# Five buffers for the last batch's layer norm, and `moe2_w_k` rebuilt by column halves

## The chip, the cores and the metric

The kernel runs on one core of a Trainium2 chip. Its engines are TensorE (PE in the profile, its weight loads PEld), VectorE (DVE), ScalarE (ACT), GpSimd (POOL) and SyncE (SP), whose queue issues nearly all DMAs. Each engine works through its own list of instructions in order; they meet only through semaphores. The metric is the time of one execution in microseconds (us) on the device; the median of several runs counts, lower is better.

## The reference, cut to what matters

Batch 4, 8 heads, 576 positions, head size 64, so the model width is 512. An attention with a decay is followed by two blocks of matrix products:

```python
x = attention(q, k, v, f)                      # (4, 576, 512) after joining the heads
h = relu(x @ w_in)                             # 512 -> 1024
u, v = h[..., :512], h[..., 512:]
v_n = (v - mean(v)) / sqrt(var(v) + 1e-6)      # layer norm over the 512 columns
v_s = einsum('ts,bsd->btd', w_spatial, v_n) + b_spatial[None, :, None]
x = (u * v_s) @ w_out                          # 512 -> 512
x_prev = x shifted by one position, zero at the start of each batch
xk = mu_k * x + (1 - mu_k) * x_prev
xr = mu_r * x + (1 - mu_r) * x_prev
k = relu(xk @ w_k)                             # 512 -> 1024
out = sigmoid(xr @ w_r) * ((k * k) @ w_v)      # 1024 -> 512
```

The inputs of the second block are `moe2_mu_k`, `moe2_mu_r`, `moe2_w_k`, `moe2_w_v` and `moe2_w_r`, those of the first `moe_w_in`, `moe_w_spatial`, `moe_b_spatial` and `moe_w_out`. The profile leaves the 2 of moe2 out: `moe_w_k` in a row is `moe2_w_k`. Matrices come in 64-bit floats, read as pairs of 32-bit integers.

## The kernel before, in words

**Order of the work.** The program gives each piece of work a due time and sorts by it (`add`, `run`, lines 612 to 619). That fixes the program order; from it a scheduler of the language, with a timeline of its own, makes each engine's fixed list, so that an instruction whose inputs and buffers come late can be placed behind later ones. An instruction given to `pin` (line 59) is never placed ahead of the one traced before it on its engine.

**First block, batch by batch.** `plan_mlp` (lines 592 to 608) plans three groups of products for a batch: `m1v` (line 499), the `v` half of x @ w_in, in five blocks of rows (four of 128, the last of 64); `m1u` (line 559), the `u` half, in 8 tiles of 128x288; `m2` (line 572), the product with `w_spatial`, also 8 tiles, each the sum of 14 matmuls (line 585): 12 on the four full row blocks `vn`, 2 on `v0`, which holds the fifth. For batch 3, the last, the 42 halves are spread over 4.0 units of time instead of 7.0, since no attention work is left.

Each row block has a layer norm in four steps. `ln1` (line 518) takes a buffer `vt` of 128x512 and a small one, `mv`, from the pool `acts`, and ScalarE reads the product out of PSUM into `vt` with a relu (line 522). `ln2` (line 525): VectorE's statistics (lines 529, 530), ScalarE's logarithm and exponential of the variance (533, 534), five small GpSimd operations that refine the result (535 to 539). `ln3` (line 541): VectorE scales `vt` in place (544), ScalarE copies it to float16 (549; 546 and 547 for the fifth block). `ln4` (line 551): VectorE takes the rest that the float16 copy leaves (557; 555 for the fifth block). `vt` comes free when `ln4` has read it. With `bufs=2` in

```python
        v = w.tile([128, 512], F32, tag="vt", bufs=2, name="vt")
        mv = w.tile([128, 4], F32, tag="mv", bufs=3, name="mv")
```

there are two `vt` and three `mv`. In the last batch the products of `m1v` lie in PSUM banks that the attention used (lines 502 to 505), two and two. The end of `m2` is line 588 on VectorE, which multiplies by `u` out of PSUM; line 590 stores the result to HBM (`gd`).

**Second weights.** `weights2` (line 665) is a generator. Each step fetches the block after next to come (512 KB, SP queue, line 93, two buffers `wst`) and rebuilds the present one: `raw_convert` (line 96) makes 32-bit floats on ScalarE (100) and VectorE (103, 107, 108), with 100 and 103 pinned; `split` (line 63) makes a high part on ScalarE (64) and the rest on VectorE (65). A fetch buffer comes free after line 108. The list of blocks is made at line 677: a block is 128 rows (`kc`) by 512 columns, so `moe_w_out` has 4, `moe2_w_k` 8, `moe2_w_r` 4 and, in a second generator, `moe2_w_v` 8 (one for each row block `fc`). For `moe2_w_k` the rows are the outer loop, the two column halves the inner one.

**The end of the batches** is in `body`. At line 819 everything up to the last batch's products is traced; `attn`, the big pool on the right, is released, the pools of the second weights are opened there, and the loop of lines 829 to 832 puts one weight block behind each 0.22 units of the last batch's steps. Then the PSUM pools and the left pools are released (line 833), and the third stage starts.

**Third stage.** 2304 tokens in five chunks of 512 (the last 256). For each chunk `m3` (line 704) multiplies the stored `gd` by `moe_w_out`, four tiles of 12 matmuls; `mix` (728) makes `xk` and `xr`, split in two; `chunk` (748) has eight products `m4(fc)` with `moe2_w_k`, each over its four row blocks and the 128 columns of `fc` (line 758), eight `m5(fc)` with `moe2_w_v` (fc is its row block) and the gate with `moe2_w_r`. The next chunk's `m3` and `mix` are interleaved as `side`. All these matmuls are recorded under line 726.

Of the kernel before, what the change touches and what calls it, by code (L numbers as in the profile page):

```python
# [7 lines left out]
F32 = mybir.dt.float32  # L8
# [13 lines left out]
KB = [(128 * c, 128) for c in range(4)] + [(512, 64)]  # L22
# [20 lines left out]
class K:  # L43
# [472 lines left out]
            self.vp[j] = self.m1p  # L516

    def ln1(self, b, j):
        w, tn = self.acts, KB[j][1]
        v = w.tile([128, 512], F32, tag="vt", bufs=2, name="vt")  # L520
        mv = w.tile([128, 4], F32, tag="mv", bufs=3, name="mv")
        self.nc.scalar.activation(v[:tn], self.vp.pop(j)[:tn], AF.Relu, scale=self.ds[:tn, 1:2])
        self.vv[j] = (v, mv)

# [87 lines left out]
    def add(self, t, prio, fn, *args):  # L612
        self.steps.append((t, prio, len(self.steps), fn, args))
# [51 lines left out]
    def weights2(self, p, names, stage, pin=False):  # L665
        nc, a = self.nc, self.a
        if not hasattr(self, "mu"):
            self.w2 = {}
            mu = self.mu = p.tile([128, 2, 2, 4], F32, name="mu")
            for i, nm in enumerate(("moe2_mu_k", "moe2_mu_r")):  # L670
                nc.sync.dma_start(mu[:, i, 0], a[nm])
                nc.vector.tensor_scalar(mu[:, i, 1], mu[:, i, 0], -1.0, 1.0, op0=ALU.mult, op1=ALU.add)
        blocks = []
        for nm in names:
            rows, cn = a[nm].shape
            self.w2[nm] = p.tile([128, 2, rows // 128, cn], F32R, name=nm)
            blocks += [(nm, kc, slice(c0, c0 + 512)) for kc in range(rows // 128) for c0 in range(0, cn, 512)]

        todo = iter(blocks)
        st = {}  # L680
        def fetch():
            x = next(todo, None)
            if x:
                nm, kc, cs = x
                st[nm, kc, cs.start] = self.raw_load(stage, nm, slice(128 * kc, 128 * kc + 128), cs, nc.sync)
        fetch()
        yield
        for nm, kc, cs in blocks:
            fetch()
            e = stage.tile([128, 512], F32, tag="we", bufs=2, name="we")  # L690
            self.raw_convert(st.pop((nm, kc, cs.start)), e, pin)
            self.split(e, self.w2[nm][:, 0, kc, cs], self.w2[nm][:, 1, kc, cs])
            yield
# [99 lines left out]
def body(tc, a, out):  # L793
    k = K(tc, a, out)
    G = k.B * k.H
    k.setup()
    k.cum()
    k.plan_attention()
    for i, t in enumerate((-4.35, -2.35) + tuple(0.6 + 0.1 * x for x in range(8))):
        k.add(t, 8, k.init, i + 1)  # L800
    add = k.add
    add(0.6, 8, k.v0_init)
    for i in range(8):
        hf, kc = 1 - i // 4, i % 4
        t = (P["w1"] if hf else P["w0"]) + P["wd"] * kc
        add(t, 7, k.wconv, i)
        if i > 2:
            add(t - 1.2, 9, k.wload, i, k.nc.sync)
        add(P["s1"] + P["sd"] * kc if hf else P["s0"] + P["sd"] * kc, 7, k.wsplit, i)
    add(P["s1"] - 0.5, 7, k.wscale, 1)  # L810
    add(P["s0"] - 0.5, 7, k.wscale, 0)
    ws = k.weights_spatial()
    for i in range(9):
        add(P["wsp"] + 0.4 * i, 7, next, ws, 0)
    end = 0
    for b in range(k.B):
        end = k.plan_mlp(b, 8 * b + 8 + P["mlp"] + (0, 0, 0.8, 0)[b], P["mlplen"] if b < 3 else 4.0)
    last = G + 1.45
    k.run(last)
    k.at.release()  # L820
    wp = k.pool("weights2", side="right")
    k.p3 = k.pool("phase3", side="right")
    wst = k.pool("wstage2", side="right")
    k.chunks = [(512 * i, min(512, 2304 - 512 * i)) for i in range(5)]
    k.x2, k.xx = {}, {}
    w2 = k.weights2(wp, ("moe_w_out", "moe2_w_k", "moe2_w_r"), wst, True)
    next(w2)
    last += 1.65
    while k.steps:
        last += 0.22  # L830
        k.run(last)
        next(w2, 0)
    for p in (k.pso, k.pst, k.pss, k.psm, k.acts, k.w):
        p.release()
    k.ps3 = k.pool("ps3", space=PSUM)
    k.p2 = k.pool("phase2", side="left")
    w2b = k.weights2(k.p2, ("moe2_w_v",), wst)
    wrest = (x for w in (w2, w2b) for x in w)
    for _ in k.m3(0):
        next(w2, 0)  # L840
    for w in range(2):
        for _ in k.mix(0, w):
            next(w2, 0)
    for _ in range(4):
        next(wrest, 0)
    for i in range(5):
        side = (x for y in ((k.m3(i + 1), k.mix(i + 1, 0), k.mix(i + 1, 1)) if i < 4 else ()) for x in y)
        n = 0
        for _ in k.chunk(i):
            next(wrest, 0)  # L850
            n += 1
            if n <= 5 or n >= 9:
                next(side, 0)
            if n == 12:
                next(side, 0)
        for _ in side:
            next(wrest, 0)
    for p in (k.ps3, k.p2, wst, k.p3, wp, k.hl, k.c):
        p.release()
# [42 lines left out]
```

## Time and profile before

| | before |
|---|---|
| median of 3 runs | 744.61 us (744.12 to 744.65) |
| profiled execution: its time | 743.56 us |
| profiled execution: span from first to last instruction | 741.7 us |
| mean granted TensorE clock | 0.973 |
| TensorE busy, share of the span | 664.9 us, 90% |
| VectorE busy | 413.7 us, 56% |
| ScalarE busy | 372.1 us, 50% |
| GpSimd busy | 153.9 us, 21% |

Times in rows are us from the start of the span. "Busy" is the union of an engine's instructions; two of them can overlap a little, so a row of 0.69 us can be followed by the next 0.60 us later. The granted clock is a share of full speed: 1.00 is 2.4 GHz, 0.50 is 1.2 GHz. A wait is put down to the instruction that released it.

### The profile page before, as it was taken

What the parts mean: (1) busy time and instruction counts of PE and PEld (TensorE: products, weight loads), DVE (VectorE), ACT (ScalarE), POOL (GpSimd) and SP (SyncE); (2) the same over time, 40 slices, a digit from 0 to 9 for tenths busy, and PEclk for the clock granted to TensorE, in tenths of its full rate; (3) what the DMA queues carried; (4) which work ended last, traced back from release to release, by engine and by line L of the source; (5) the groups of instructions that cost most, each with busy time, mean ns of one, the idle gap of its engine ahead of it and who ended that gap; (6) DMA issues with size and microseconds to landing.
All of it is one profiled execution on the core that took longest, in us unless ns stands there. A gap on an engine that the chain in (4) does not pass through costs nothing.

```text
span 741.7 us, 11689 instructions
## 1 busy us (share of the span) xinstructions
PE 664.9 (90%) x4166; PEld 457.6 (62%) x4166; DVE 413.7 (56%) x1122; ACT 372.1 (50%) x762; POOL 153.9 (21%) x356
## 2 busy tenths in 40 slices
PE   1488886999989899999998489999999999999997
PEld 0234343466655565456655267788888888888896
DVE  6868776874465555553118789886226412731342
ACT  4547776595446744454317448655335322622431
POOL 8122434443335223442212000000000000000000
PEclk9999798999999999999999599999999999999999
DMA  7977566444461434400115464441000100010010
GB/s 239 256 207 184 139 119 183 150 96 104 104 167 52 115 73 107 84 18 18 50 49 196 144 198 153 142 115 47 10 29 15 57 1 15 0 57 1 0 57 30
DMA packets 73616, 70.07 MB, mean 94 GB/s; under 512 B 50883, under 2 KB 51555, under 8 KB 73558
## 3 DMA queue, kind: packets, MB, share of 16 engines
q1 hardware_dynamic: 73126, 68.14, 33.5%
q10 hardware_dynamic: 432, 1.18, 0.4%
q8 instruction: 33, 0.54, 0.3%
q14 instruction: 25, 0.20, 0.1%
HBM read 43.78 MB, written 9.79 MB: 72 GB/s over the span
## 4 chain that ended last, share of the span: by engine, by line
PE 56%; DMA 21%; DVE 8%; ACT 5%; POOL 4%; issue 3%; SPq 2%; POOLq 0%; ACTq 0%; DVEq 0%
PE m L726 37%; DMA sr<-rd 5%; DMA qT<-nq 3%; PE m1v L514 3%; PE o L377 3%; PE s L288 3%; PE t L321 3%; PE m L585 3%; PE o L359 2%; DMA wst<-in_moe_w_k_dram 2%; PE m1u L568 2%; DMA rd<-r 2%; POOL xo L399 2%; DMA knat<-in_k_dram 2%; DVE junk L297 1%
## 5 line engine op out<-in xcount | busy, mean ns | idle before, releaser
L726 PE MATMUL m<-xx,moe_w_k 128*128 128x512 f32 (+1 forms) x480 | 106.0, 369 | 0.4 <-ACT x L721 0.4
L297 DVE CUSTOM_DVE_ANT_0 junk<-s,mask 128x512 bf16<-128x512 f32 (+4 forms) x160 | 76.0, 475 | 52.9 <-PE s L288 47.4
L726 PE MATMUL m<-moe_w_v,k 128*128 128x512 f32 x432 | 104.2, 390 | 0.0
L726 PEld LDWEIGHTS m<-xx,moe_w_k 128*128 128x128 f32 x480 | 83.9, 188 | 16.9 <-ACT x L721 0.9
L325 ACT ACTIVATE e<-t,qa 128x512 f32<-128x512 f32 (+1 forms) x128 | 72.3, 590 | 40.8 <-PE t L321 39.8
L726 PEld LDWEIGHTS m<-moe_w_v,k 128*128 128x128 f32 x432 | 80.7, 188 | 17.0
L330 POOL TENSOR_SCALAR_AFFINE_SELECT e<-e 128x128 f32<-128x128 f32 (+1 forms) x160 | 49.7, 326 | 117.5 <-ACT e L325 116.5
L762 DVE TENSOR_TENSOR tmp<-tmp 128x512 f32<-128x512 f32 (+1 forms) x40 | 25.5, 638 | 86.9 <-ACT tmp L761 86.7
L288 PE MATMUL s<-kT,qT 128*128 128x512 f16 (+2 forms) x192 | 54.7, 299 | 14.4 <-DMA kT<-nk 7.9
L585 PE MATMUL m<-wspT,vn 128*128 128x288 f16 x384 | 59.4, 297 | 4.1 <-ACT vn L549 2.4
L321 PE MATMUL t<-qA,kA 69*128 69x512 f16 (+2 forms) x192 | 50.4, 291 | 10.8 <-ACT e L325 7.7
L514 PE MATMUL m1v<-win,xt 128*128 128x512 f16 x240 | 58.2, 388 | 1.8 <-ACT xt L402 1.7
L761 ACT ACTIVATE tmp<-m 128x512 f32<-128x512 f32 (+1 forms) x40 | 22.2, 557 | 71.6 <-PE m L726 71.3
L568 PE MATMUL m1u<-xt,win 128*128 128x288 f16 x384 | 55.4, 286 | 2.3 <-ACT u L570 2.3
L377 PE MATMUL o<-e,v 128*64 128x64 f32 (+4 forms) x384 | 53.8, 412 | 4.0 <-POOL e L330 1.9
L726 PE MATMUL m<-gh,moe_w_out 128*128 128x512 f32 (+1 forms) x240 | 54.0, 374 | 3.6 <-DVE u L588 2.6
L288 PE MATMUL s<-kA,qA 67*128 67x512 f16 (+2 forms) x192 | 50.3, 300 | 4.6 <-DMA kA<-cumd 3.9
L321 PE MATMUL t<-qT,kT 128*128 128x512 f16 (+2 forms) x192 | 52.0, 289 | 0.0
L726 PE MATMUL m<-moe_w_r,xx 128*128 128x512 f32 x216 | 51.2, 394 | 0.0
L726 PEld LDWEIGHTS m<-gh,moe_w_out 128*128 128x128 f32 x240 | 42.1, 188 | 13.4 <-DVE u L588 2.9
L585 PEld LDWEIGHTS <-vn 128*128 128x128 f16 x384 | 37.2, 101 | 19.3 <-ACT vn L549 3.0
L726 PEld LDWEIGHTS m<-moe_w_r,xx 128*128 128x128 f32 x216 | 40.4, 187 | 9.9
(155 smaller groups left out, 1036.3 us busy)
## 6 DMA issues: line engine op xcount, KB each, us to landing
knat<-in_k_dram SPq DMA_DIRECT2D x16, 320.0 KB
v<-in_v_dram SPq DMA_DIRECT2D x20, 256.0 KB
sr<-rd SPq DMA_DIRECT2D x32, 144.0 KB
gd<-u SPq DMA_DIRECT2D x16, 288.0 KB
out_dram<-o SPq DMA_DIRECT2D x18, 256.0 KB
qnat<-in_q_dram SPq DMA_DIRECT2D x14, 320.0 KB
g<-gd SPq DMA_DIRECT2D x16, 256.0 KB
wst<-in_moe_w_k_dram SPq DMA_DIRECT2D x8, 512.0 KB
```

What stands on the lines that cost most here:

```text
L288: self.nc.tensor.matmul(s[:, o:o + n], self.tok(qn, p, h, 128 * ib - 64, 128)[0:r], self.tok(kn, p, h, k0, n)[0:r], start=(j == 0), stop=( ...
L297: self.nc.vector.tensor_tensor_reduce(out=self.junk[r0:, 0:n], in0=self.s[u % 2][r0:, o:o + n], in1=self.mask[r0:, m0:m0 + n], op0=ALU.add ...
L321: self.nc.tensor.matmul(t[:, o:o + n], self.tok(kn, p, h, 128 * c, 128)[0:r], self.tok(qn, p, h, q0, n)[0:r], start=(j == 0), stop=(j == 1))
L325: self.nc.scalar.activation(self.e[g][:, 512 * u:512 * u + n], t[:, 0:n], AF.Exp, scale=self.qa[p][:, 5:6])
L330: self.nc.gpsimd.affine_select(out=e, in_=e, pattern=[[1, n]], compare_op=ALU.is_ge, fill=0.0, base=0, channel_multiplier=-1)
L377: self.chain(self.nc.tensor.matmul(o[r, 448 + f:448 + q1], v[:, c, pr, r], self.e[2 * p + h][:, off:off + q1 - f], start=(c == 0), stop=(c ...
L514: nc.tensor.matmul(self.m1p, xt[:, xs, 128 * j:128 * j + 128], self.win[:, ws, kc, 512:1024], start=(kc == 0 and n == 0), stop=(kc == 3 an ...
L568: self.nc.tensor.matmul(o, self.win[:, ws, kc, fs], self.xt[(4 * b + kc) % 8][:, xs, ts_], start=(kc == 0 and n == 0), stop=(kc == 3 and n ...
L585: nc.tensor.matmul(o, pairs[n][0], pairs[n][1], start=(n == 0), stop=(n == 13))
L726: self.nc.tensor.matmul(out, l, r, start=(first and j == 0), stop=(last and j == len(pairs) - 1))
L761: nc.scalar.activation(tmp[:, 0:n], ps[:, 0:n], AF.Relu)
L762: nc.vector.tensor_tensor(tmp[:, 0:n], tmp[:, 0:n], tmp[:, 0:n], ALU.mult)
```

## The change

`ln1` takes its two buffers for the last batch from a pool `lnp` of its own, with five `vt` and six `mv`; the other batches go on with two and three in `acts`. The pool is opened on the left side behind the release of the attention's pool, and released with the others ahead of the third stage. In `weights2` the loops of the block list change places: column halves outside, rows inside. Of the four matrices only `moe2_w_k` has more than one column block, so only its order changes.

```diff
     def ln1(self, b, j):
-        w, tn = self.acts, KB[j][1]
-        v = w.tile([128, 512], F32, tag="vt", bufs=2, name="vt")
-        mv = w.tile([128, 4], F32, tag="mv", bufs=3, name="mv")
+        tn = KB[j][1]
+        w, n = (self.acts, 2) if b < self.B - 1 else (self.lnp, 5)
+        v = w.tile([128, 512], F32, tag="vt", bufs=n, name="vt")
+        mv = w.tile([128, 4], F32, tag="mv", bufs=n + 1, name="mv")
...
-            blocks += [(nm, kc, slice(c0, c0 + 512)) for kc in range(rows // 128) for c0 in range(0, cn, 512)]
+            blocks += [(nm, kc, slice(c0, c0 + 512)) for c0 in range(0, cn, 512) for kc in range(rows // 128)]
...
     k.at.release()
+    k.lnp = k.pool("norms", side="left")
     wp = k.pool("weights2", side="right")
...
-    for p in (k.pso, k.pst, k.pss, k.psm, k.acts, k.w):
+    for p in (k.pso, k.pst, k.pss, k.psm, k.lnp, k.acts, k.w):
         p.release()
```

## Rows read from the trace of the kernel before

**Rows 1.** The page's part 1: busy us (share of the span) xinstructions

```profile
PE 664.9 (90%) x4166; PEld 457.6 (62%) x4166; DVE 413.7 (56%) x1122; ACT 372.1 (50%) x762; POOL 153.9 (21%) x356
```

**Rows 2.** Stretches: length, busy us of each engine (x), PEclk, DMA share, GB/s

```profile
403.60:419.10 15.50, 4.53 (x25) 2.31 (x23) 11.34 (x21) 7.86 (x16) 3.92 (x14) 0.67 0.51 169
...
448.00:476.40 28.40, 26.97 (x115) 21.03 (x114) 27.05 (x47) 21.94 (x40) 0.65 (x2) 1.00 0.39 128
390.00:472.60 82.60, 65.60 (x345) 47.57 (x344) 71.55 (x132) 53.42 (x103) 7.39 (x26) 0.90 0.51 167
...
500.00:741.00 241.00, 237.85 (x1105) 196.78 (x1103) 94.92 (x176) 89.17 (x165) 0.39 (x2) 1.00 0.07 25
```

**Rows 3.** Waits from 403.5 to 419.2: us in total, times, longest

```profile
PE m L585 <- DVE v L555: 7.7, 1, 7.7
...
PE m L585 <- ACT vn L549: 2.4, 2, 1.9
...
PE m L585 <- DVE vn L557: 0.9, 1, 0.9
```

**Rows 4.** Timeline of PE: start us, us, line, operation [idle before <-releaser]

```profile
390.49 2.75 PE L514 MATMUL m1v<-win,xt 128*128 128x512 f16 x12
...
403.55 1.65 PE L585 MATMUL m<-wspT,vn 128*128 128x288 f16 x12
...
420.77 3.04 PE L585 MATMUL m<-wspT,vn 128*128 128x288 f16 x12 [0.47 <-DVE u L588]
...
426.66 1.63 PE L585 MATMUL m<-wspT,vn 128*128 128x288 f16 x12
...
432.30 1.63 PE L585 MATMUL m<-wspT,vn 128*128 128x288 f16 x12
...
436.79 11.47 PE L726 MATMUL m<-gh,moe_w_out 128*128 128x512 f32 x48 [2.61 <-DVE u L588]
448.09 3.82 PE L726 MATMUL m<-xx,moe_w_k 128*128 128x512 f32 x16
...
476.44 1.08 PE L726 MATMUL m<-moe_w_v,k 128*128 128x512 f32 x4
```

**Rows 5.** Timeline of ACT: the last batch's reads into `vt`

```profile
389.75 1.27 ACT L522 ACTIVATE vt<-m1v,ds 128x512 f32<-128x512 f32 x2 [2.70 <-PE m1v L514]
...
398.33 0.68 ACT L522 ACTIVATE vt<-m1v,ds 128x512 f32<-128x512 f32 x1
...
399.29 0.70 ACT L522 ACTIVATE vt<-m1v,ds 128x512 f32<-128x512 f32 x1
...
409.48 0.67 ACT L522 ACTIVATE vt<-m1v,ds 64x512 f32<-64x512 f32 x1
```

**Rows 6.** Timeline of DVE: the last batch's layer norm

```profile
397.23 0.69 DVE L557 TENSOR_TENSOR vn<-vt,vn 128x512 f16<-128x512 f32 x1
...
407.97 0.69 DVE L557 TENSOR_TENSOR vn<-vt,vn 128x512 f16<-128x512 f32 x1
...
411.24 0.68 DVE L529 BATCH_NORM_STATS2 st<-vt 64x6 f32<-64x512 f32 x1
...
416.09 0.54 DVE L544 TENSOR_SCALAR vt<-vt,mv 64x512 f32<-64x512 f32 x1 [0.90 <-POOL mv L539]
418.42 0.69 DVE L555 TENSOR_TENSOR v<-vt,v 64x512 f16<-64x512 f32 x1 [1.79 <-ACT v L546]
```

**Rows 7.** Timeline of POOL: pairs of the layer norm's small operations

```profile
403.94 1.12 POOL L536 TENSOR_TENSOR mv<-mv 128x1 f32<-128x1 f32 x2
405.02 0.34 POOL L537 TENSOR_TENSOR mv<-mv 128x1 f32<-128x1 f32 x2
```

**Rows 8.** Timeline of DVE: last step of rebuilt weight blocks

```profile
430.06 0.69 DVE L65 TENSOR_TENSOR moe_w_k<-we,moe_w_k 128x512 fp32r<-128x512 f32 x1 [0.26 <-ACT moe_w_k L64]
...
440.74 0.69 DVE L65 TENSOR_TENSOR moe_w_k<-we,moe_w_k 128x512 fp32r<-128x512 f32 x1
...
471.86 0.69 DVE L65 TENSOR_TENSOR moe_w_v<-we,moe_w_v 128x512 fp32r<-128x512 f32 x1
```

## The prediction, made before the changed kernel was seen

> **What bounds the kernel now.** I began with the engines' shares: TensorE is busy for 90% of the span, VectorE for 56% [rows 1]. That is an average over stages with different limits, so I next looked at stretches. From 500 us to the end TensorE is busy for 237.85 of 241 us at a granted clock of 1.00 [rows 2]: a wait taken away ahead of that point moves all of it forward, and nothing in the change touches it. The loose time lies where the last batch's layer norm ends: from 403.6 to 419.1 TensorE works for 4.53 of 15.50 us, with a mean granted clock of 0.67 [rows 2]. The waits of that stretch name the cause: 7.7 us once for the copy `v` of the fifth row block, 2.4 and 0.9 us for `vn` [rows 3].
>
> The timelines show why `v` is late. All first products of the last batch were through TensorE by 390.49 + 2.75 = 393.24 [rows 4], yet ScalarE read only two of them at 389.75; the next two followed at 398.33 and 399.29, the fifth at 409.48 [rows 5]. `vt` has two buffers, and each later read comes just behind the end of a reader of the buffer it needs: VectorE's `vn` of block 0 ends at 397.23 + 0.69 = 397.92, that of block 2 at 407.97 + 0.69 = 408.66 [rows 6]. So five blocks go in three rounds; the last ends with line 555 at 418.42 + 0.69 = 419.11 [rows 6], and TensorE resumes at 419.17 with its second-stage products (line 585).
>
> **The change, part by part.**
>
> *1. Five buffers for `vt`, six for `mv`.* No instruction is added, removed or resized; the same 5 reads, 5 statistics, 25 small GpSimd operations, scalings and splits are only let go earlier. The reads of blocks 2 and 3 can follow the first two at once, that of block 4 once its product is there (393.24). One round took 419.11 - 409.48 = 9.6 us for block 4 alone, so with block 4 read at about 393.3 its end lies near 403, and later where three more blocks share the engines. TensorE begins the second stage at 403.55 [rows 4]. I call the lateness of the first unbroken group d.
>
> Second stage now: 436.79 - 403.55 = 33.24 us until the first product with `moe_w_out` [rows 4]. It has 8 groups of 14 matmuls. Three groups in a row went from 426.66 to 432.30, 1.88 us each, including their waits for VectorE [rows 4]: 8 x 1.88 = 15.0 us. The handover behind them, 2.61 us of idle until VectorE's last line 588 [rows 4], I leave as it is. The clock's loss is in the difference: 12 matmuls took 3.04 us from 420.77, behind the long idle stretch, and 1.63 us from 426.66 [rows 4]; without the idle stretch the slow ones go too.
>
> For d, the lower end is 0 (403 is ahead of 403.55). The upper end comes from GpSimd: a pair of line 536 took 1.12 us at 403.94, beside VectorE's work, a pair of line 537 only 0.34 us at 405.02 [rows 7]. If all 25 of its operations took 0.56 us, its chain from about 392.4 would end at 406.4, and the fifth block's tail, 419.11 - 416.09 = 3.0 us [rows 6], would end at 409.4, 5.9 us late; TensorE has the parts of two groups that need no `v` to do meanwhile, 2 x 1.63 = 3.3 us, so d = 2.6. I take the middle, d = 1.3. The Trainium skill, "SBUF — State Buffer", section "Who interferes with whom", says that a VectorE instruction with two SBUF inputs and a GpSimd instruction that reads SBUF hold the same port one after the other, each for its whole length. The pair at 1.12 us agrees, the pair at 0.34 us met a gap; by that rule in full d would be 2.6 us and the sum below 1.3 us worse.
>
> Term 1: 33.24 - (15.0 + 2.6 + 1.3) = **14.3 us** earlier at the start of the third stage, 422.5 instead of 436.79.
>
> *2. The pool of its own.* It is opened on the left, where only a stage of the first weights had been, released long before; it adds no wait that I can place. It is released with the others, and the third stage's first writers of that side wait for the second stage anyway (the handover above). I cost it at 0.
>
> *3. `moe2_w_k` by column halves.* The eight blocks, their 512 KB transfers, two fetch buffers and conversions are the same; only which block is which changes. Product 0 of chunk 0 (line 758) needs all four row blocks of the first columns: so far the seventh block, in future the fourth. The third stage takes 448.09 - 436.79 = 11.3 us for `moe_w_out`, then `moe2_w_k` is wanted: at 422.5 + 11.3 = 433.8. The fourth block was ready at 430.06 + 0.69 = 430.75, the seventh at 440.74 + 0.69 = 441.43 [rows 8]. In the old order TensorE would wait from 433.8, less 9 matmuls on row blocks 0 to 2 (some 2.1 us), up to 5.5 us. In the new order it is covered by 3 us, even if the blocks come no earlier. The second halves are wanted four products later. Alone this part would be worth nothing (in the kernel before, the seventh block is there 6.7 us ahead of 448.09); here it keeps term 1, cost 0.
>
> *4. What is late next: `moe2_w_v`.* The first product with it begins at 476.44 [rows 4], its first block was ready at 471.86 + 0.69 = 472.55 [rows 8]. Moved by term 1 it is wanted at 476.44 - 14.3 = 462.1. VectorE converts every block, and in that time also mixes and splits for chunk 0: 71.55 us busy in the 82.60 us from 390.00 [rows 2]. Without any idle time it would be done at 461.6, just in time; with all its idle time except the two waits of the fifth block, 0.90 + 1.79 = 2.7 us [rows 6], at 469.9. I take the share of its densest stretch, 27.05 of 28.40 us [rows 2], since the same work is pushed together: 71.55 / 0.952 = 75.1, so 465.1. Term 4: 465.1 - 462.1 = **3.0 us** given back. TensorE could fill some of that with products 5 to 7 of chunk 0, if the program's order on it allows.
>
> Sum: 14.3 - 3.0 = 11.3 us. The profiled execution took 743.56 us (span 741.70 and 1.86 around it); 743.56 - 11.3 = 732.3. The median of the runs is 744.61, 1.05 above the profiled one, so I forecast **733.3 us**.
>
> **Rivals.**
>
> A. *VectorE stays the bound.* Only the 2.7 us go; the first `moe2_w_v` block is ready at 469.9 and TensorE, with its 4 us of slack used up, follows at once: 476.44 - 469.9 = 6.5 us, 738.1. For it: VectorE is 95% busy from 448 to 476.4 [rows 2], and conversions are limited by two fetch buffers. Against it: before 448 it has gaps, and block conversions that stood behind the layer norm move up too.
>
> B. *GpSimd's chain stretches* as in the upper end of d: 1.3 us less gain, 734.6. For it the 1.12 us pair, against it the 0.34 us pairs [rows 7]. The port rule of the Trainium skill cited above would give this outcome.
>
> C. *Nothing moves.* The instruction order on ScalarE and VectorE is fixed at build time; if blocks 2 to 4 stay behind weight conversions there, the extra buffers stand empty: 744.6. Against it: the reads follow the releases within 0.4 to 0.8 us [rows 5, 6], so it was the buffers.
>
> D. *Slower.* Conversions of weights are pinned behind what was written ahead of them on their engine. If the three layer-norm blocks set free are all put in front of conversions, VectorE delays those by three times its statistics, scaling and split, 0.68 + 0.54 + 0.69 = 1.9 us [rows 6], together 5.7 us. The first `moe2_w_v` block would come at 472.55 + 5.7 = 478.3, and the wait moves there: 1.8 us later than now, 746.4. It decides once that block comes after 476.4. Against it: those conversions now wait for the same layer-norm blocks, and later.
>
> **How the numbers follow.** Forecast 0.55, A 0.25, B 0.08, C 0.05, D 0.07. A measurement of this kernel can tell 0.2%, 1.5 us, from no change. Faster by more: forecast, A and B, 0.88; within it: C, 0.05; slower: D, 0.07. The range starts at d = 0 with nothing given back, 33.24 - 17.6 = 15.6 us, 729.0, and goes past A to 740.5, since A's idle time and d's upper end can come together (738.1 + 1.3) and a little of the second halves may be late; C and D, 0.12, and some tail stay out.
>
> **What would show it.** Right: the five reads of `vt` stand within some 5 us of 389.7; the wait for `v` is gone or under 3 us, and the granted clock stays at 1.00 through 405 to 425; the first product with `moe_w_out` comes at 421 to 425; the first with `moe2_w_k` 11 to 12 us later without a wait for its weights; the first with `moe2_w_v` near 465, with VectorE over 90% busy ahead of it; from there to the end the time is as now. Wrong: the fifth read still behind 405 (C), a `moe_w_out` start beyond 428 (term 1 mis-sized), or idle TensorE time over 6 us between 434 and 470 with `moe2_w_v`, `xx` or `gh` as its releaser (A, and at the extreme D).

## The result and the profile after

The kernel after takes **734.25 us** (median of 9 runs, 732.63 to 738.76), the one before on the same chip 744.12 (9 runs, 739.82 to 747.01): a ratio of 0.9877, with a 95% interval of 0.9847 to 0.9906. That is 9.9 us saved; the forecast was 11.3.

The page of after, its first lines (columns as in [rows 1]):

```profile
span 733.2 us, 11687 instructions
PE 663.8 (91%) x4166; PEld 457.9 (62%) x4166; DVE 415.5 (57%) x1122; ACT 372.1 (51%) x762; POOL 156.7 (21%) x356
```

No matmul and no VectorE, ScalarE or GpSimd operation was taken out (the counts are those of [rows 1]); the same work has fewer gaps. From the layer norm on, lines stand one further down than before (555 is now 556, 588 is 589, 726 is 727). To compare executions I count from one **anchor**: the start of the last first products, `m1v` x12, at 390.49 us before [rows 4] and at 387.44 after. Up to there every engine's list is the same in both kernels, so the 3.05 us between the two anchors come from the execution, not from the change. TensorE's timeline of after (idle time and releaser in brackets):

```profile
387.44 2.75 PE L514 MATMUL m1v<-win,xt 128*128 128x512 f16 x12
...
400.44 0.90 PE L586 MATMUL m<-wspT,vn 128*128 128x288 f16 x6 [0.57 <-ACT u L571]
...
402.98 2.27 PE L586 MATMUL m<-wspT,vn 128*128 128x288 f16 x16 [1.06 <-ACT u L571]
406.02 0.66 PE L586 MATMUL m<-wspT,v 128*128 128x288 f16 x4 [0.77 <-DVE v L556]
407.77 1.63 PE L586 MATMUL m<-wspT,vn 128*128 128x288 f16 x12 [1.09 <-DVE u L589]
...
415.36 2.62 PE L586 MATMUL m<-wspT,vn 128*128 128x288 f16 x12 [2.29 <-DVE u L589]
...
423.33 11.47 PE L727 MATMUL m<-gh,moe_w_out 128*128 128x512 f32 x48 [0.99 <-DVE u L589]
434.63 3.03 PE L727 MATMUL m<-xx,moe_w_k 128*128 128x512 f32 x12
...
445.18 1.78 PE L727 MATMUL m<-xx,moe_w_k 128*128 128x512 f32 x6 [2.24 <-ACT xx L64]
...
474.36 5.76 PE L727 MATMUL m<-moe_w_r,xx 128*128 128x512 f32 x24
479.96 1.09 PE L727 MATMUL m<-moe_w_v,k 128*128 128x512 f32 x4
```

The wait for `v` fell from 7.7 us [rows 3] to 0.77. The third stage (`moe_w_out`) starts 35.9 us behind the anchor instead of 46.3. What remains is spread: some 1 us each for PSUM banks that ScalarE (line 571) and VectorE (line 589) have to read first, 0.77 us for `v`, 2.29 us for one more line 589, and later 2.24 us for a split `xx` of ScalarE. ScalarE's reads of `vt` in after answer to [rows 5]:

```profile
386.70 2.42 ACT L523 ACTIVATE vt<-m1v,ds 128x512 f32<-128x512 f32 x4 [2.70 <-PE m1v L514]
...
390.24 0.68 ACT L523 ACTIVATE vt<-m1v,ds 64x512 f32<-64x512 f32 x1
```

Four follow one another without a gap and the fifth comes 3.5 us behind the first; before, the five spanned 19.7 us. The fifth block's end in after, GpSimd's last operation and VectorE's last:

```profile
400.04 0.52 POOL L540 TENSOR_TENSOR mv<-mv 64x1 f32<-64x1 f32 x1
```

```profile
405.27 0.69 DVE L556 TENSOR_TENSOR v<-vt,v 64x512 f16<-64x512 f32 x1
```

Stretches (start and end; length; busy us of PE, PEld, DVE, ACT and POOL with counts; granted clock; DMA share; GB/s): first the anchor to the third stage in before; then, of after, the same, a part of it, and two behind it.

```profile
390.49:436.79 46.30, 30.73 (x198) 20.27 (x196) 37.34 (x72) 24.55 (x52) 6.92 (x25) 0.82 0.54 179
```

```profile
387.44:423.33 35.89, 28.55 (x198) 19.55 (x196) 30.27 (x60) 21.07 (x47) 9.11 (x25) 0.95 0.58 186
415.00:420.00 5.00, 4.64 (x25) 3.15 (x25) 4.25 (x8) 1.44 (x3) 0.00 (x0) 0.66 0.70 211
434.60:474.30 39.70, 36.78 (x145) 28.53 (x144) 34.01 (x59) 27.14 (x50) 0.65 (x2) 0.91 0.42 131
445.00:454.00 9.00, 8.14 (x22) 5.95 (x23) 6.99 (x12) 4.08 (x8) 0.00 (x0) 0.62 0.36 116
```

The two spans that the change can touch, in us, in four executions; TensorE's busy and idle time make up the first:

| kernel | anchor to third stage | TensorE busy, idle in it | granted clock | third stage to the end |
|---|---|---|---|---|
| before | 46.30 | 30.73, 15.57 | 0.82 | 304.91 |
| before, again (e4) | 46.65 | 30.65, 16.00 | 0.82 | 304.30 |
| after | 35.89 | 28.55, 7.34 | 0.95 | 309.87 |
| after, again (e3) | 35.77 | 29.65, 6.12 | 0.90 | 306.32 |

So the stretch up to the third stage gives 10.7 us on the mean (46.5 less 35.8). Of these, 9.1 are idle time and 1.6 is busy time, that is, clock. Behind the third stage's start 5.0 us go back in one execution of after and 2.0 in the other (against 304.9 and 304.3).

### The profile page after: what moved, and what is told of

Read it like the earlier page. It is cut to its first block, busy times and chain, and to the rows that moved or that the text cites. A ratio compares the mean times of both kernels' runs of the same rounds, so it can differ in the third digit from the quotient of the medians.

```text
span 733.2 us, 11687 instructions
## 1 busy us (share of the span) xinstructions
PE 663.8 (91%) x4166; PEld 457.9 (62%) x4166; DVE 415.5 (57%) x1122; ACT 372.1 (51%) x762; POOL 156.7 (21%) x356
## 4 chain that ended last, share of the span: by engine, by line
PE 53%; DMA 18%; DVE 11%; ACT 6%; POOL 5%; issue 4%; SPq 2%; DVEq 0%; POOLq 0%; ACTq 0%
PE m L727 34%; DMA sr<-rd 4%; PE m L586 4%; PE t L321 3%; PE o L377 3%; PE o L359 3%; PE s L288 3%; DMA wst<-in_moe_w_k_dram 2%; PE m1v L514 2%; DVE junk L297 2%; PE m1u L569 2%; DMA wst<-in_moe_w_v_dram 2%; DMA rd<-r 2%; POOL xo L399 2%; ACT junka L69 1%
## 5 line engine op out<-in xcount | busy, mean ns | idle before, releaser
L288 PE MATMUL s<-kT,qT 128*128 128x512 f16 (+2 forms) x192 | 54.6, 297 | 15.8 <-DMA kT<-nk 7.9
L586 PE MATMUL m<-wspT,vn 128*128 128x288 f16 x384 | 57.5, 291 | 5.2 <-DVE u L589 3.4
L727 PE MATMUL m<-gh,moe_w_out 128*128 128x512 f32 (+1 forms) x240 | 56.5, 386 | 1.7 <-DVE u L589 1.0
L727 PEld LDWEIGHTS m<-gh,moe_w_out 128*128 128x128 f32 x240 | 44.0, 196 | 12.0 <-ACT x L722 1.4
L586 PEld LDWEIGHTS <-vn 128*128 128x128 f16 x384 | 36.6, 99 | 19.3 <-issue 7.3
```

Source lines behind the costliest of these rows:

```text
L288: self.nc.tensor.matmul(s[:, o:o + n], self.tok(qn, p, h, 128 * ib - 64, 128)[0:r], self.tok(kn, p, h, k0, n)[0:r], start=(j == 0), stop=( ...
L586: nc.tensor.matmul(o, pairs[n][0], pairs[n][1], start=(n == 0), stop=(n == 13))
L727: self.nc.tensor.matmul(out, l, r, start=(first and j == 0), stop=(last and j == len(pairs) - 1))
```

## The experiments

Two theories stood at the start: that the five buffers do it alone, and that the new order of `moe2_w_k` keeps part of the gain. Later ones asked why the second stage gave less than forecast, and what takes time back behind it. They ran in three groups, each on a chip of its own with the kernel before beside it: 740.85 us for e1 to e4, 742.59 for e5 to e8, 741.73 for e9 to e12. So totals of different groups are compared by their ratio to the kernel before, which is 0.9877 for the change; times within an execution are from one trace each.

**e1: the buffers alone.** In the kernel after, the old order:

```diff
-blocks += [(nm, kc, slice(c0, c0 + 512)) for c0 in range(0, cn, 512) for kc in range(rows // 128)]
+blocks += [(nm, kc, slice(c0, c0 + 512)) for kc in range(rows // 128) for c0 in range(0, cn, 512)]
```

> Only the five buffers; moe2_w_k is rebuilt in the old order. Theory (each part needs the other): the third stage starts as early as with the whole change, 35.9 us behind the last batch's last first products instead of 46.3, but TensorE then waits for the seventh block of moe2_w_k, 3 to 5 us, so the whole is 4 to 6 us faster than before and 4 to 6 slower than the change. Rival (the buffers do it all, the order of blocks is idle): within 1.5 us of the whole change, no wait for moe2_w_k.

Measured: 733.38 us, ratio 0.9886 (0.9847 to 0.9925), as fast as the whole change, so the theory was wrong and the rival right. The third stage starts 36.6 us behind the anchor, and from there to the end it takes 306.2. VectorE's row of the seventh weight block and TensorE's row of the wait in that place, in e1:

```profile
440.74 0.69 DVE L65 TENSOR_TENSOR moe_w_k<-we,moe_w_k 128x512 fp32r<-128x512 f32 x1
```

```profile
443.60 1.66 PE L727 MATMUL m<-xx,moe_w_k 128*128 128x512 f32 x6 [1.70 <-ACT xx L64]
```

The seventh block is ready at 441.43, TensorE goes on at 443.60, and it waited for `xx`, not for the weights: the first products with `moe2_w_k` are taken row block by row block as `xx` arrives, and its last row blocks come later than the weights in either order.

**e2: the order alone.** In the kernel before, only the line of e1 in its new form.

> Only the order of the moe2_w_k blocks; two vt buffers in every batch. Theory: nothing, within 1.5 us of the kernel before, since the seventh block was there 6.7 us ahead of its first use; the third stage starts 46 to 47 us behind the last first products. Rival (an earlier first half lets other products go ahead and helps by itself): 3 us or more faster.

Measured: 740.85 us, ratio 0.9998 (0.998 to 1.0017), the third stage 46.8 us behind the anchor. No effect. With e1: the order of the halves is idle, and the whole gain is the buffers'.

**e3 and e4: the two kernels again**, unchanged, for the spread between executions.

> The changed kernel once more, for a second trace. In the first pair of traces 3.05 of the 8.5 us of difference lay ahead of the first instruction that the change can touch. Theory (that part is the spread of single executions): from the last batch's last first products to the end it takes 344 to 347 us again, and the point itself lies anywhere from 386 to 391 us. Rival (the earlier part is really faster): the point lies at 387 to 388 again and that of the kernel before stays at 390 to 391.

> The kernel before once more, for a second trace. Theory: 350 to 352 us from the last batch's last first products to the end, the point itself anywhere from 386 to 391 us. Rival: the point lies at 390 to 391 as in the first trace.

Measured: 732.53 us, ratio 0.9891 (0.9843 to 0.9939), and 741.49 us, 1.0 (0.9971 to 1.0029). From the anchor to the end it took 342.1 us in e3, less than the 344 to 347 expected, and 350.95 in e4; the anchors lay at 388.31 and 389.95. Stretches of e3: the anchor to the third stage, a low point of the clock in it, and the stretch that answers to 445 to 454 of after.

```profile
388.31:424.08 35.77, 29.65 (x197) 19.96 (x196) 30.24 (x60) 20.30 (x45) 10.06 (x25) 0.90 0.57 186
409.30:412.30 3.00, 2.83 (x12) 1.72 (x12) 2.35 (x5) 0.96 (x2) 0.00 (x0) 0.50 0.70 150
445.70:454.70 9.00, 8.31 (x34) 6.19 (x35) 8.51 (x15) 6.55 (x13) 0.00 (x0) 1.00 0.40 133
```

The same program has its clock at 0.50 (1.2 GHz) in the second stage here and at 1.00 behind it; after has 0.66 and 0.62 in other places. Up to the third stage e3 has 1.1 us more busy time (29.65 against 28.55) and 1.2 less idle time, from the same lists of instructions.

**e5: no refinement on GpSimd.** The kernel leaves out four of the five operations for the last batch.

```diff
+if b == self.B - 1:
+    g.tensor_scalar(y, y, VS, None, op0=ALU.mult)
+    return
```

> The changed kernel, with four of the five small GpSimd operations of a row block left out in the last batch (the refinement of the inverse deviation; one scaling stays). Theory (GpSimd's 25 operations, stretched beside VectorE's instructions with two inputs, set the last normalised block): line 556 ends 2 to 4 us earlier and the third stage starts at 32.5 to 34.5 us behind the last batch's last first products instead of 35.8 to 35.9. Rival (the order on ScalarE and VectorE sets it, GpSimd has slack): 35.3 us or later.

Measured: 727.54 us, ratio 0.9798 (0.9746 to 0.985). The anchor to the third stage in e5:

```profile
387.66:420.38 32.72, 26.45 (x197) 18.95 (x195) 29.42 (x60) 20.02 (x45) 3.93 (x5) 1.00 0.61 195
```

The end of line 556 (559 in e5) moved from 18.5 to 16.4 us behind the anchor, and the third stage came at 32.72, about where the forecast of 32.0 had it. But the idle time, 32.72 - 26.45 = 6.27 us, is as in e3 (6.12). What this execution gains over e3 in this stage is the clock: 26.45 us is what the stage's matmuls take at 1.00 (26.44 in e12, the other execution at 1.00). This gives the clock's price in the other executions: before 30.73 - 26.45 = 4.3 us, after 2.1, e3 3.2. Whether the clock held because of the missing operations isn't shown: e11 and e12 below differ by it with the same lists.

**e6: later weight conversions**, so that none stands in front of the second stage's `u` on VectorE.

```diff
+n = 0
...
-        next(w2, 0)
+        n += 1
+        if n < 5 or last > 38.05:
+            next(w2, 0)
+for _ in w2:
+    pass
```

In after, the 2.29 us wait of TensorE has this on VectorE:

```profile
412.05 0.43 DVE L103 TENSOR_SCALAR wst<-wst 128x512 int32<-128x512 int32 x1 [1.69 <-DMA wst<-in_moe_w_k_dram]
...
414.45 0.43 DVE L103 TENSOR_SCALAR wst<-wst 128x512 int32<-128x512 int32 x1 [0.92 <-DMA wst<-in_moe_w_k_dram]
414.80 0.51 DVE L589 SCALAR_TENSOR_TENSOR u<-m,sw,u 128x288 f32<-128x288 f32 x1
```

VectorE, 84% busy in this stage (30.27 of 35.89 us), stood idle at a conversion whose transfer had not landed, with a ready line 589 behind it and TensorE behind that.

> The changed kernel, with the conversions of moe2_w_k and moe2_w_r pinned behind more of the last batch's multiplications by u (line 589): blocks 5 to 16 are traced later, so VectorE does not stand at a conversion that waits for its transfer while a PSUM bank waits for it. Theory (that standing and the fall of the clock behind it cost the second stage some 2 us): no wait of TensorE of over 1 us for line 589 inside the second stage, the third stage starts 1 to 2.5 us earlier, and the whole is 0 to 2.5 us faster than the change, less what the later blocks cost. Rival (the weights are the tighter chain): TensorE waits for moe2_w_k or its split in the third stage, and the whole is 2 us or more slower.

Measured: 731.04 us, ratio 0.9847 (0.9805 to 0.9889). The same rows in e6:

```profile
416.08 0.52 DVE L589 SCALAR_TENSOR_TENSOR u<-m,sw,u 128x288 f32<-128x288 f32 x1 [1.20 <-PE m L586]
416.51 0.42 DVE L103 TENSOR_SCALAR wst<-wst 128x512 int32<-128x512 int32 x1
```

Now VectorE waits for TensorE there, and TensorE's longest wait for line 589 in the stage is 1.09 us. The third stage came at 34.05 instead of 35.8, with 5.72 us idle and 28.33 busy: against after that is 1.6 us less idle time. Against e3 it is 0.4 less, and the rest is clock; in e3 the 2.29 us wait did not occur, with the same lists, so the standing at the transfer is a loss of some executions only. The total has an interval that overlaps that of the change.

**e7: late splits of `g` behind `xx`.** `g` is the stored `gd` fetched for a chunk, `gh` its split. On ScalarE the last two splits of `g` for the second chunk are put behind the last split of `xx` for the first.

```diff
-self.nc.scalar.copy(hi, src)
+self.hi = self.nc.scalar.copy(hi, src)
...
+if (i, w, kc) == (0, 0, 3):
+    self.xlast = self.hi
...
+if i == 1 and kc > 1:
+    self.tc.add_manual_dep(self.hi.ins, self.xlast.ins.name, ...)
```

In after, ScalarE stands at a split of `g` during TensorE's 2.24 us wait, with the splits of `xx` behind it:

```profile
443.99 0.62 ACT L64 CAST gh<-g 128x512 fp32r<-128x512 f32 x1 [1.34 <-DMA g<-gd]
444.51 1.66 ACT L64 CAST xx<-tmp 128x512 fp32r<-128x512 f32 x3
```

Again an engine stands at an instruction whose transfer is late, and what TensorE wants next is queued behind it.

> The changed kernel, with the last two splits of the second chunk's gd put behind the last split of the first chunk's xx in ScalarE's order. Theory (the give-back is ScalarE standing at a split whose transfer is late, 1.8 to 2.2 us of TensorE, and in some executions a fall of the clock of 3.7 us): the wait of the products with moe2_w_k for xx is gone or under 0.7 us, the granted clock stays at 1.00, 1 to 4 us faster than the change. Rival (VectorE's total work is the bound): the wait comes back under another name, within 1 us of the change.

Measured: 732.99 us, ratio 0.9876 (0.9836 to 0.9915). ScalarE and TensorE in that place in e7:

```profile
441.85 0.61 ACT L64 CAST xx<-tmp 128x512 fp32r<-128x512 f32 x1
442.36 0.61 ACT L64 CAST gh<-g 128x512 fp32r<-128x512 f32 x1
443.24 0.62 ACT L64 CAST gh<-g 128x512 fp32r<-128x512 f32 x1 [0.27 <-DMA g<-gd]
```

```profile
445.68 0.96 PE L729 MATMUL m<-gh,moe_w_out 128*128 128x512 f32 x3 [0.17 <-DVE gh L65]
```

The wait is gone, and from the third stage to the end it takes 305.03 us, against 309.87 and 306.32 in after and 304.9 and 304.3 in before. TensorE's idle time in that stretch is 4.91 us, as in before (5.28 and 4.47), where after has 7.08 and e3 6.32; in e10 below, which lacks this edit but waits only 0.44 us for `xx`, it is 4.93. So this wait, with the clock that sometimes falls behind it, is what was given back. Against e3 the stretch is only 1.3 us shorter, and the total is that of the change (0.9876), not the 1 to 4 us faster that were expected.

**e8: lighter rebuild.** Line 107 is left out in all 24 blocks of the second block's weights: VectorE has some 14 us less to do.

```diff
-def raw_convert(self, st, out, pin=False):
+def raw_convert(self, st, out, pin=False, full=True):
...
-nc.vector.scalar_tensor_tensor(ei, ei, 3, low, ALU.logical_shift_left, ALU.bitwise_or)
+if full:
+    nc.vector.scalar_tensor_tensor(ei, ei, 3, low, ALU.logical_shift_left, ALU.bitwise_or)
...
-self.raw_convert(st.pop((nm, kc, cs.start)), e, pin)
+self.raw_convert(st.pop((nm, kc, cs.start)), e, pin, False)
```

> The changed kernel, with line 107 left out of the conversion of all 24 blocks of the second weights: 24 x 0.6 = 14 us less work on VectorE. The prediction's step 4 (VectorE's share of the time up to the first product with moe2_w_v is the bound): 3 us or more faster. Rival (waits at late transfers on ScalarE and VectorE are the bound, not their work): under 1.5 us faster.

Measured: 735.75 us, ratio 0.992 (0.9893 to 0.9947), not faster. The 65 us from 70 us behind the anchor, in after and in e8:

```profile
457.44:522.44 65.00, 64.73 (x282) 52.53 (x281) 53.88 (x97) 41.04 (x71) 0.19 (x1) 1.00 0.33 106
```

```profile
462.23:527.23 65.00, 65.00 (x285) 53.03 (x284) 39.06 (x70) 34.46 (x60) 0.19 (x1) 1.00 0.19 63
```

TensorE is busy nearly all the time in both, with VectorE at 53.88 us or at 39.06. The give-back lies ahead of this stretch, so the whole of the third stage has to be looked at: from its start to the end VectorE is busy for 143.94 us in e8 and for 158.69 in after, and yet TensorE's idle time is 6.29 us against 7.08 (6.32 in e3). VectorE's share of work is not what bounds this stage.

**e9: three buffers** instead of five: `(self.lnp, 3)` for `(self.lnp, 5)`.

> The changed kernel with three vt and four mv for the last batch instead of five and six. Theory (each missing buffer sends a block into a later round): blocks 3 and 4 are read when blocks 0 and 1 are done, some 10 to 12 us behind the last first products, line 556 ends 20 to 23 us behind them instead of 18.5 to 19.7, the third stage starts at 37 to 40 us, 2 to 4 us slower than the change and 5 to 7 faster than before. Rival (GpSimd's chain paces the blocks anyway, three buffers are enough): line 556 within 1 us of the change, the third stage at 36 us or earlier.

Measured: 736.77 us, ratio 0.9918 (0.9871 to 0.9964). ScalarE's reads of `vt`, and TensorE's wait for `v`, in e9:

```profile
386.91 1.84 ACT L523 ACTIVATE vt<-m1v,ds 128x512 f32<-128x512 f32 x3 [2.70 <-PE m1v L514]
396.88 0.69 ACT L523 ACTIVATE vt<-m1v,ds 128x512 f32<-128x512 f32 x1
399.95 0.68 ACT L523 ACTIVATE vt<-m1v,ds 64x512 f32<-64x512 f32 x1
```

```profile
411.26 1.14 PE L586 MATMUL m<-wspT,v 128*128 128x288 f16 x4 [3.19 <-DVE v L556]
```

Three reads at once, two later, each behind a release (the `vn` of blocks 0 and 1, done at 396.05 and 397.85; their `mv` were free by 394.4, so it is `vt` that counts): the third stage 41.27 us behind the anchor, half way between 46.5 and 35.8, and so is TensorE's idle time (11.81, between 15.8 and 6.7). That is even later than the 37 to 40 expected, and line 556 ended at 23.6 instead of 20 to 23. This is the plainest evidence for the number of buffers as the cause, by the stage; the total, some 3 us slower than the change by its ratio, has an interval that overlaps.

**e10: three operations on GpSimd** instead of five for the last batch, with the scale (`VS`, 512) moved into ScalarE's exponential (`lvs` holds its logarithm).

```diff
+if b == self.B - 1:
+    nc.scalar.activation(y, y, AF.Exp, scale=-0.5, bias=self.lvs[:tn])
+    g.tensor_scalar(var, var, 1e-6, -0.5 / VS ** 2, op0=ALU.add, op1=ALU.mult)
+    g.tensor_scalar(tmp, var, y, y, op0=ALU.mult, op1=ALU.mult)
+    g.tensor_scalar(y, tmp, 1.5, y, op0=ALU.add, op1=ALU.mult)
+    return
```

> The changed kernel, the refinement of the last batch in three GpSimd operations a row block instead of five (the factor 512 goes into ScalarE's exponential as a bias, the square into an operation with two scalars): nothing is left out. Theory (GpSimd's chain sets the last normalised block, by the number of its operations): 15 operations lie between the 25 of the change and the 5 of the run without refinement, so line 556's counterpart ends about 17.2 to 18.5 us behind the last first products and the third stage starts at 33.3 to 35 us; 1 to 3 us faster than the change. Rival (the gain without refinement came from another order on VectorE and ScalarE): no order, anywhere from 32.5 to 37 us, with GpSimd's end earlier and line 556's not.

Measured: 735.19 us, ratio 0.9908 (0.9876 to 0.9941); third stage at 35.57, no gain, where 33.3 to 35 was expected. The counterpart of line 556 ends 18.95 us behind the anchor (18.5 in after), and GpSimd's 15 operations are busy for 8.85 us, the 25 of after for 9.11. A pair on GpSimd and VectorE's instructions about it, in e10 (VectorE's lines here stand 8 further down than in after):

```profile
395.52 2.75 POOL L540 TENSOR_SCALAR mv<-mv 128x1 f32<-128x1 f32 x2 [0.94 <-ACT mv L538]
```

```profile
397.45 0.69 DVE L566 TENSOR_TENSOR vn<-vt,vn 128x512 f16<-128x512 f32 x1
398.55 1.00 DVE L553 TENSOR_SCALAR vt<-vt,mv 128x512 f32<-128x512 f32 x2 [0.41 <-POOL mv L541]
```

The pair ends at 398.27, when VectorE's unbroken run ends (397.45 + 0.69 = 398.14). Fewer operations, each held longer: the count is not the price.

**e11 and e12: combinations.** e11 is e6 with e10; e12 adds e7.

> Three GpSimd operations a block and the later pins of the moe2_w_k conversions together. Theory (the two waits lie one behind the other in the second stage): the gains add up, the third stage starts at 31.5 to 33.5 us behind the last first products, 3 to 5 us faster than the change, 727 to 731 us. Rival (the weights become the bound once the second stage is shorter): third stage as early, but TensorE waits 1.5 us or more for moe2_w_k or moe2_w_v, no faster than either alone.

> As before with the second chunk's late gd splits behind the first chunk's last xx split as well: all three together. Theory (the three waits are separate): no wait of TensorE over 1.3 us between the last first products and the second chunk, clock at 1.00 but for the second stage's start, 4 to 7 us faster than the change, 726 to 730 us. Rival (with the weights later, gh is late instead and the order has no worth): within 1 us of the run without it.

Measured: e11 730.3 us, ratio 0.9842 (0.9808 to 0.9876); e12 732.91 us, 0.9864 (0.9831 to 0.9897). Their stretches, the anchor to the third stage and 3 us from 21 us behind the anchor, e11 first:

```profile
388.44:422.48 34.04, 28.11 (x197) 19.64 (x195) 28.24 (x56) 19.81 (x44) 8.97 (x15) 0.95 0.55 175
409.40:412.40 3.00, 2.92 (x13) 1.86 (x13) 2.25 (x5) 0.87 (x2) 0.00 (x0) 0.54 0.70 161
```

```profile
391.97:423.90 31.93, 26.44 (x197) 18.87 (x196) 28.14 (x56) 19.66 (x44) 8.72 (x15) 1.00 0.59 185
413.00:416.00 3.00, 3.00 (x27) 2.38 (x26) 2.17 (x5) 0.62 (x1) 0.00 (x0) 1.00 0.77 168
```

Up to the third stage the two have the same lists on TensorE, VectorE, ScalarE and GpSimd, and nearly the same idle time (5.93 and 5.49 us). Yet the clock fell to 0.54 in one and stayed at 1.00 in the other, which makes 1.7 us of busy time. e12 reached the forecast's 32.0 for this stage, but took 308.5 us from there to the end, so the total did not follow. e11's 730.3 us lies in the 727 to 731 expected, but by its ratio it is 2.6 us below the change and not 3 to 5, and its third stage comes at 34.04 us and not at 31.5 to 33.5; e12 missed its 726 to 730. The order of `gh` was worth nothing here: e11, without it, shows no wait for `xx` behind the third stage's start and takes 308.4 us from there. What makes this stretch 2.4 us longer than in e6 (306.04) is TensorE's busy time for the same 1368 matmuls, 302.72 and 302.84 us against 300.15, at a granted clock of 1.00 in all three: between 500 and 700 us a matmul with `moe2_w_k` takes 395 ns on the mean in e10, e11 and e12, and 392 in e6 and e9. The slower three carry e10's edit; why they are slower is open, and their totals hold some 2.5 us of it.

e6 and e11 are 0.3% below the change by their ratios (0.9847 and 0.9842 against 0.9877), with overlapping intervals; whether they beat it stays open. So does a third fetch buffer for the weights or for `g`, which would go at both remaining waits directly: no run has it.

## Why the prediction was right, and where not

- **The cause: right.** Five buffers let the reads go at once, the wait for `v` nearly vanished, and the third stage started earlier in every execution with five. e1, e2 and e9 carry this. That its start, 423.33, lies inside the 421 to 425 of "What would show it" is luck: 3.05 us of it are the earlier anchor. Counted from the anchor it came at 35.9 us, where 30.5 to 34.5 had been forecast.
- **Term 1: right in kind, too large.** 14.3 us were forecast, 10.7 measured. The forecast left 46.30 - 14.3 = 32.0 us, which at the full clock (26.45 busy) means 5.5 idle. The shortfall of 3.8 us is the clock for the most part, 2.1 (after) and 3.2 (e3), and idle time, 1.8 (7.34) and 0.6 (6.12).
  - *The clock.* The step "without the idle stretch the slow ones go too" failed. The long idle stretch went, but waits of 0.6 to 2.3 us were left, and behind them the clock fell again, to 0.66 in after and 0.50 in e3, where "What would show it" had 1.00 throughout. Its loss went from 4.3 to 2.1 and 3.2, not to 0.
  - *d.* I had 0 to 2.6 us and took 1.3. In after the third group begins at 407.77; less two groups of 1.88 and counted from 403.55 - 3.05 = 400.50, d was 407.77 - 3.76 - 400.50 = 3.5, above the upper end. Two things were missing. The fifth block's tail, from GpSimd's last operation (400.56) to the end of line 556 (405.27 + 0.69 = 405.96), took 5.4 us, not the 3.0 it takes alone, since it shares VectorE and ScalarE with conversions and splits. And the unbroken groups were broken once, 2.29 us, by VectorE at a late transfer, in after though not in e3 (e6). Part of this came back in the handover, left at 2.61, now 0.99 (1.73 in e3).
- **Part 2, the pool: right** as far as can be seen. No row of after shows a wait for it.
- **Part 3, the order of `moe2_w_k`: wrong.** That "it keeps term 1" rested on all four row blocks of the weights being wanted at the stage's start. They are wanted one by one as `xx` comes (e1), and the old order costs nothing. TensorE did turn to `moe2_w_k` 11.3 us behind `moe_w_out`, without a wait for weights, as forecast.
- **Term 4: the size in range, the cause wrong.** 3.0 us were forecast; 5.0 and 2.0 went back. But TensorE stood for `moe2_w_v` for only 0.27 us, later on. The forecast shifted the old order of TensorE's list; the scheduler made another, with all products of the first chunk with `moe_w_k` and half of those with `moe_w_r` first, so `moe_w_v` was reached at 479.96, later than before, and the want at 462.1, on which the term rests, never arose. That its size fits is luck. VectorE was 86% busy ahead of it (34.01 of 39.70 us) rather than the 95% that my division assumed. e8 refutes the division itself. The give-back is the wait for `xx` behind a late `g` (2.24 us, e7) and the clock behind it, 0.62 in 445 to 454 in one execution and 1.00 in the other.
- **The sum** came out near the measurement, 11.3 against 9.9 us, and that is luck in part. From the anchor to the end the two executions of after are 5.5 and 8.9 us shorter than those of before, 7.2 on the mean (10.7 less the 3.5 given back); with e1 and e2, whose order of blocks has no effect, the means of three differ by 7.9 (343.6 against 351.4). The medians differ by 9.9 (7.0 to 11.4 by the interval), and by 8.3 in the group of e3. So the mechanism gives some 3 to 4 us less than forecast, nearly all of it in term 1, and the spread of the medians covers part of that. The anchors themselves lie between 385.5 and 392.2 us over all kernels, with lists that are the same up to there but for one extra early instruction in e10 to e12 (and GpSimd operations that change places beside it).
- **The rivals.** A is refuted by e8. B named a real thing: GpSimd's operations were stretched, and e5 without most of them has a ratio of 0.9798, against 0.9891 for e3, with intervals that just overlap; in the second stage of its one trace the gain over e3 is the clock, not less waiting. C and D did not happen.

## What to carry to other kernels

Count the rounds in which a row of blocks goes through its buffers before costing anything else: five blocks in two buffers were three rounds, in three buffers two, in five buffers one, and each step was seen in the stage's time (46.5, 41.3 and 35.8 us). When a long wait goes, do not price its slow clock as gone: it can fall again behind the short waits that stay, in one execution and not in the next. And look for what is late next at the head of each in-order queue, where an instruction stands for a transfer with ready work behind it, rather than in an engine's busy share.

## What was not expected of the hardware

A GpSimd operation of 128x1 can last until a run of several VectorE instructions is over (spans on GpSimd are rough in this profile). GpSimd and VectorE in after, in one place:

```profile
392.09 1.51 POOL L539 TENSOR_SCALAR mv<-mv 128x1 f32<-128x1 f32 x1
393.68 0.19 POOL L540 TENSOR_TENSOR mv<-mv 128x1 f32<-128x1 f32 x1
```

```profile
392.09 0.52 DVE L545 TENSOR_SCALAR vt<-vt,mv 128x512 f32<-128x512 f32 x1
392.54 0.68 DVE L107 SCALAR_TENSOR_TENSOR we<-we,wst 128x512 int32<-128x512 int32 x1
393.14 0.41 DVE L103 TENSOR_SCALAR wst<-wst 128x512 int32<-128x512 int32 x1
393.47 0.16 DVE L531 BATCH_NORM_AGGREGATE mv<-st 64x2 f32<-64x6 f32 x1
```

The operation begins with VectorE's first instruction and ends at 393.60, between the ends of the third (393.55) and the fourth (393.63), not with the first (392.61). The next one, in VectorE's pause behind 393.63, took 0.19 us. In e5 one lasted 2.62 us, in e10 a pair 2.75. The Trainium skill, "SBUF — State Buffer", section "Who interferes with whom", has the engine that issues first hold a shared port for its whole instruction while the other is blocked. These rows agree that the two keep each other out; they add that GpSimd got no turn between the first three VectorE instructions.

The other is the clock: with the same lists and nearly the same idle time it fell in e11 and not in e12, and in different places in after and e3. Its share of a forecast of this size, 2 to 3 us, can be bounded but was not predictable from the program.
